# A spectral mixing kernel on one core: three weight transfers in one piece instead of three uneven ones

## The chip, the cores and the metric

The kernel runs on one core of a Trainium2 chip. The metric is the device time of one execution in microseconds (us); lower is better. The engines named below are TensorE (PE in the profile, PEld for its weight loads), VectorE (DVE), ScalarE (ACT), GpSimd (POOL) and SyncE (SP). Transfers between the chip's memory and the core run on 16 DMA engines, whichever engine issues them.

## The reference

Two stages, here cut to what they compute. There are B = 8 batches, S = 576 positions, 8 heads of 64 columns (D = 512 columns together) and 64 modes.

```
scores = q k^T / 8, masked: heads 0-3 see the last 32 positions,
                            heads 4-7 the earlier positions that are equal modulo 32
x = softmax(scores) v, heads side by side                    # [8, 576, 512]
X = rfft(x, axis=1)[:, :64]
Y[b, m, :] = X[b, m, :] @ (w_r[m] + i w_i[m])                # 64 complex matrices of 512 x 512
u = x + irfft(Y, n=576)
out = u + relu(u @ w_ch)                                     # float32
```

The weights w_r and w_i are 2 x 64 x 512 x 512 float32 numbers, 134 MB of the 163 MB that are read from memory. Each is used once, for eight batches.

## The kernel before

All transfers of inputs are issued by POOL, which turns float32 into float16 on the way. The attention's inputs come first and in between; the weights follow in an order that is written out (`ORDER`): 56 modes of the second half of the input channels, 48 modes of the first half, then the remaining 8 and 16. `w_fetch` loads two modes of one half at a time into a tile `wt` of 128 partitions: partitions 0 to 63 take the real parts (w_r, line 185), partitions 64 to 127 the imaginary parts (w_i, line 185), each as one transfer of 64 partitions x 2 modes x 2048 numbers, 512 KB as written. The first transfers of each half and the last four modes are loaded one mode at a time (line 189). There are five rotating buffers for these tiles and three more in places that are free for a while.

`i` is the position in `ORDER`, counted in modes, and steps by two. At three of these positions, 44, 74 and 102, the kernel before loads the real parts in three transfers (line 181) that share out the 64 partitions as the table `UNEVEN` says: 35, 18 and 11; 5, 33 and 26; 18, 35 and 11.

POOL's transfers take turns on eight semaphores, so that a transfer is issued after the one eight places before it has landed; a transfer into a buffer that was in use also waits for TensorE to be done with that buffer (`mode`, line 564). After every second mode, `mode` calls `w_fetch` for the next pair.

Attention is worked on in eight batches, first its strided heads, then its local heads, with the first modes spread between the local heads' steps. While the 48 modes that follow are worked off, `turn` and `premix` transpose x and multiply it by w_ch ahead of time, since u @ w_ch = x @ w_ch + irfft(Y) @ w_ch. In the last 24 modes one step of a list `late` follows each mode: `renew` adds what the first three of the four groups of 16 modes bring to x and to x @ w_ch (lines 894, 906 and 707 on TensorE, lines 250 and 911 on ScalarE and VectorE). When the last mode is done, the fourth group is added (line 965), and the rows go out through ScalarE, VectorE and SP.

The order of the work on each engine is the order in which it is written; no scheduler changes it.

Of the kernel before, what the change touches and what calls it, by code (L numbers as in the profile page):

```python
# [56 lines left out]
def kernel(  # L57
# [10 lines left out]
    nc = tc.nc  # L68
# [79 lines left out]
    SPLIT1, SPLIT0 = 56, 48  # L148
    ORDER = [(1, m) for m in range(SPLIT1)] + [(0, m) for m in range(SPLIT0)]
    ORDER += [(1, m) for m in range(SPLIT1, NM)] + [(0, m) for m in range(SPLIT0, NM)]  # L150
    UNEVEN = {44: (35, 18, 11), 74: (5, 33, 26), 102: (18, 35, 11)}
    w_tiles = []
    w_chs = {}
    w_ch = big.tile([128, 4, DM], F16, name="w_ch")
# [1 line left out]
    def w_fetch(n=1):  # L156
        for _ in range(n):
            i = len(w_tiles)
            if i >= 2 * NM:
                return  # L160
            half, m = ORDER[i]
            if i // 2 in GUEST:
                wt = big.tile([128, 2, 4, DM], F16, tag=GUEST[i // 2], name="wt")
            else:
                wt = pw.tile([128, 2, 4, DM], F16, tag="w", name="wt")
            single = []
            for ri, src in enumerate((moe_w_r, moe_w_i)):
                dst = wt[ds(64 * ri, 64)]
                rows = src[m : m + 2, ds(256 * half, 256), :].rearrange(
                    "m (p c) e -> p m (c e)", c=4  # L170
                )
                dst = dst.rearrange("p m c e -> p m (c e)")


                ones = range(2)
                if ri and not m:
                    ones = [1]
                elif i in UNEVEN and not ri:
                    a = 0
                    for n in UNEVEN[i]:  # L180
                        nc.gpsimd.dma_start(dst[a : a + n], rows[a : a + n])
                        a += n
                    continue
                elif i < 2 * NM - 4:
                    nc.gpsimd.dma_start(dst, rows)  # L185
                    continue
                single += [(j, ri, dst[:, j], rows[:, j]) for j in ones]
            for _, _, to, rows in sorted(single, key=lambda x: x[:2]):
                nc.gpsimd.dma_start(to, rows)
            w_tiles.extend((wt[:, 0], wt[:, 1]))  # L190
# [362 lines left out]
    def mode(slot, m):  # L553
# [17 lines left out]
        if m % 2 and (slot or m // 2 not in GUEST):  # L571
            w_fetch()
# [144 lines left out]
    strided_tokens()  # L717
    load_str(2, 2)
    w_fetch()

    def str_front(b):
# [35 lines left out]
    for b in range(B):  # L757
        if b in (1, 3):
            load_str(b + 3, 2)
        load_loc(*[(), (), (), (), (0,), (1, 2), (3,), (4, 5)][b])  # L760
        w_fetch([2, 1, 1, 1, 1, 1, 0, 0][b])
        front = str_front(b + 1) if b + 1 < B else loc_front(0)
        for t in range(6):
            str_scores(b, t)
            if b > 0:
                if t < 2:
                    str_values(b - 1, 4 + t)
                elif t == 2:
                    dft(b - 1, 1)
            if t >= 2:  # L770
                str_values(b, t - 2)
            for w in front[SPLIT[t] : SPLIT[t + 1]]:
                w()
        if b == 1:
            nc.vector.memset(PL[:, 0:PS0], 0.0)
            fourier(0)
# [8 lines left out]
    for b in range(B):  # L785
# [12 lines left out]
        n = 0  # L798
        nm = NMODES[b]
        for mi in range(nm):  # L800
# [3 lines left out]
            n = upto  # L804
# [66 lines left out]
    n = 0  # L871
    for m in range(SPLIT0):
# [4 lines left out]
        n = upto  # L877
# [125 lines left out]
    n = 0  # L1003
    NL = len(rest) - 2
    for i, (slot, m) in enumerate(rest):
# [4 lines left out]
        n = upto  # L1010
# [76 lines left out]
```

## Time and profile before

| | us |
|---|---|
| median of three runs | 434.12 (433.67 to 434.50) |
| profiled execution | 434.12 |
| its span, from the first to the last instruction | 432.3 |

| engine | busy us (share of the span) |
|---|---|
| TensorE, matmuls | 348.7 (81%) |
| VectorE | 236.3 (55%) |
| ScalarE | 203.5 (47%) |
| POOL | 111.0 (26%) |

The core read 162.8 MB and wrote 9.4 MB; the DMA engines moved 91.78 MB as written, since the weights shrink to float16 on the way.

How to read it: the slices cut the span in 40 equal parts of 10.8 us, and a digit is the busy share in tenths. The chain is followed back from the last instruction, at each step to what released it. A line of the POOL timeline gives the start of an issue, how long POOL was at it, what it moves, and in brackets how long POOL stood still before it and what ended that. The trace also has a record for each packet and for each landing of a transfer on one of the 16 DMA engines.

### The profile page before, as it was taken

The numbers are of one execution on the slowest core, as the hardware profiler recorded it, in microseconds if no ns is written. First come the engines' busy times: TensorE is split into PE (matmuls) and PEld (weight loads), VectorE is DVE, ScalarE is ACT, GpSimd is POOL, SyncE is SP. The second block draws the span as 40 slices with busy tenths as digits, with TensorE's granted clock in tenths as the row PEclk, the third lists the DMA queues.
The fourth block names the chain that finished last, engine by engine and source line by source line (L and its number), as shares of the span: only waits on it lengthen the run. The fifth ranks groups of instructions, "written<-read, shape, count | busy, mean of one in ns | idle before, by whom it ended". The sixth has DMA issues, their size and how long they took to land.

```text
span 432.3 us, 12283 instructions
## 1 busy us (share of the span) xinstructions
PE 348.7 (81%) x5420; PEld 240.0 (56%) x5420; DVE 236.3 (55%) x461; ACT 203.5 (47%) x357; POOL 111.0 (26%) x197
## 2 busy tenths in 40 slices
PE   2978788779897888898477878787887888988994
PEld 2867676558676666666344545455554544444331
DVE  3887878844533424533104244865783474444685
ACT  1776778636545345546141222522441453432773
POOL 8333332323332222232222222222223222110000
PEclk9997999968968869969655578999898989899997
DMA  8999999999999999999999999999999999991698
GB/s 151 211 211 213 214 212 212 212 210 212 214 212 213 214 213 214 212 213 214 211 214 214 213 213 215 213 213 213 213 214 211 214 213 214 213 200 30 219 355 300
DMA packets 30900, 91.78 MB, mean 212 GB/s; under 512 B 4416, under 2 KB 5184, under 8 KB 30848
## 3 DMA queue, kind: packets, MB, share of 16 engines
q0 software_dynamic: 25120, 81.28, 95.1%
q1 hardware_dynamic: 5216, 9.52, 6.2%
q8 instruction: 42, 0.69, 0.6%
q10 hardware_dynamic: 512, 0.21, 0.2%
q14 instruction: 10, 0.08, 0.0%
HBM read 162.83 MB, written 9.44 MB: 398 GB/s over the span
## 4 chain that ended last, share of the span: by engine, by line
DMA 59%; PE 21%; DVE 9%; ACT 5%; issue 4%; POOL 1%; DVEq 0%; POOLq 0%; ACTq 0%
DMA wt<-in_moe_w_i_dram 46%; DMA wt<-in_moe_w_r_dram 11%; DVE kz L282 3%; PE y L564 2%; DVE xb L240 2%; PE v L942 2%; PE u L952 2%; PE sc L531 2%; ACT X L250 2%; PE v L965 1%; DMA ring<-in_q_dram 1%; PE tp L412 1%; ACT v L250 1%; DVE rec L239 1%; ACT PL L377 1%
## 5 line engine op out<-in xcount | busy, mean ns | idle before, releaser
L564 PE MATMUL y<-X,wt 128*128 128x16 f16 (+1 forms) x2048 | 82.4, 192 | 37.1 <-DMA wt<-in_moe_w_i_dram 35.3
L564 PEld LDWEIGHTS <-wt 128*128 128x128 f16 (+1 forms) x2048 | 72.9, 102 | 52.0 <-issue 45.3
L185 POOL DMA_DIRECT2D wt<-in_moe_w_r_dram x59 | 34.6, 586 | 128.2 <-PE y L564 50.9
L185 POOL DMA_DIRECT2D wt<-in_moe_w_i_dram x60 | 35.3, 588 | 66.9 <-DMA wt<-in_moe_w_i_dram 47.6
L673 ACT ACTIVATE v<-sc 128x512 f16<-128x512 f32 x32 | 19.1, 597 | 67.5 <-PE sc L664 67.4
L488 ACT ACTIVATE PL<-sc 128x480 f16<-128x480 f32 (+1 forms) x48 | 27.4, 579 | 33.1 <-PE sc L474 32.7
L664 PE MATMUL sc<-w_cp,xT 128*128 128x512 f16 x128 | 40.0, 440 | 1.3 <-DVE xT L637 1.3
L674 DVE COPY xo<-tp 128x512 f16<-128x512 f16 x32 | 22.1, 691 | 34.1 <-PE tp L672 34.0
L240 DVE TENSOR_TENSOR xb<-av,rec 90x256 f16<-90x256 f32 (+2 forms) x80 | 36.0, 450 | 2.8
L239 DVE RECIPROCAL rec<-av 90x4 f32<-90x4 f32 (+2 forms) x80 | 14.6, 183 | 35.2 <-PE av L503 24.8
L419 DVE COPY qT<-tp 128x576 f16<-128x576 f16 x16 | 12.0, 758 | 39.1 <-PE tp L412 36.2
L911 DVE TENSOR_TENSOR xo<-u,xo 128x1024 f16<-128x1024 f32 x16 | 19.6, 1225 | 16.9 <-PE u L707 16.9
L250 ACT ACTIVATE v<-tp 128x640 f16<-128x640 f16 (+1 forms) x24 | 19.4, 807 | 18.8 <-PE tp L446 16.3
L412 PE MATMUL tp<-cI_s,ring 64*64 64x64 f16 x864 | 25.1, 205 | 1.2 <-DVE qT L419 0.6
L377 ACT ACTIVATE PL<-sc 90x360 f16<-90x360 f32 (+1 forms) x48 | 22.7, 490 | 7.1 <-PE sc L370 6.5
L250 ACT ACTIVATE v<-v 128x1024 f16<-128x1024 f32 x16 | 16.4, 1023 | 19.6 <-PE v L707 19.6
L987 DVE TENSOR_TENSOR osb<-u,rl 128x1024 f32<-128x1024 f32 (+1 forms) x21 | 22.2, 1071 | 5.5 <-PE u L965 3.4
L458 PE MATMUL sc<-cMl_s,cI_s 128*128 128x480 f16 (+1 forms) x48 | 21.1, 440 | 3.2 <-ACT X L250 1.6
L412 PEld LDWEIGHTS <-ring 64*64 64x64 f16 x864 | 19.6, 118 | 6.2 <-issue 2.8
L275 PE MATMUL tp<-cI_s,ring 72*128 72x72 f16 x256 | 15.6, 208 | 8.6 <-DMA ring<-in_v_dram 6.9
L531 PEld LDWEIGHTS <-xb 108*128 108x128 f16 (+2 forms) x176 | 15.3, 106 | 12.0 <-DVE xb L240 7.2
L979 ACT ACTIVATE rl<-v 128x1024 f32<-128x1024 f32 (+1 forms) x21 | 18.8, 901 | 6.6 <-PE u L965 4.1
(135 smaller groups left out, 705.5 us busy)
## 6 DMA issues: line engine op xcount, KB each, us to landing
wt<-in_moe_w_i_dram POOLq DMA_DIRECT2D x60, 512.0 KB, 18.8
wt<-in_moe_w_r_dram POOLq DMA_DIRECT2D x59, 512.0 KB, 18.0
out_dram<-osb SPq DMA_DIRECT2D x15, 512.0 KB, 3.2
ring<-in_v_dram POOLq DMA_DIRECT2D x8, 288.0 KB, 13.3
ring<-in_q_dram POOLq DMA_DIRECT2D x8, 288.0 KB, 13.6
ring<-in_k_dram POOLq DMA_DIRECT2D x8, 288.0 KB, 13.1
ring<-in_v_dram POOLq DMA_DIRECT2D x3, 512.0 KB, 14.7
ring<-in_q_dram POOLq DMA_DIRECT2D x3, 512.0 KB, 14.6
```

What stands on the lines that cost most here:

```text
L185: nc.gpsimd.dma_start(dst, rows)
L240: nc.vector.tensor_tensor(out=dst, in0=val.rearrange("p h (q c) -> p h c q", c=4), in1=rec[0:n, 0:pieces] .to_broadcast((n, pieces, 64)) . ...
L250: nc.scalar.activation(out=out, in_=in_, func=ACTF.Copy)
L377: nc.scalar.activation(out=PS[0:n, ds(POFF[t], 4 * n)], in_=scp[0:n, 0 : 4 * n], func=ACTF.Exp, scale=SCALE,)
L412: nc.tensor.transpose(tp[ds(64 * hp, 64), ds(64 * i, 64)], qn[ds(64 * hp, 64), ds(64 * (9 * g + i), 64)], idn[ds(64 * hp, 64), ds(64 * hp, ...
L458: nc.tensor.matmul(scp[:, 0 : n * times].rearrange("p (h x) -> p h x", h=times), idn, mask_rows("cMl", n, times), start=True, stop=False,)
L488: nc.scalar.activation(out=dst, in_=src, func=ACTF.Exp, scale=SCALE)
L531: nc.tensor.matmul(xp[:, ds(192 * cp, 192)].rearrange("p (f m) -> p f m", f=3), xb[b][0:n, base + t, ds(128 * cp, 128)], F[0:n, :, t, :], ...
L564: nc.tensor.matmul(yv[:, mi, e, :], wt[pr, XC[c], ds(128 * e, 128)], Xh[half][pr, c, :, :, m], start=(c == 0), stop=(c == 3),)
L664: nc.tensor.matmul(vp, xT[:, ch], w_chs["cp"][:, ch, :], start=(ch == 0), stop=(ch == 3),)
L674: nc.vector.tensor_copy(out=xo.rearrange("p (h q c) -> p h q c", h=2, c=4), in_=tp[:, 0:512].rearrange("p (h c q) -> p h q c", h=2, c=4),)
L987: nc.vector.tensor_tensor(out=osb[:, j], in0=up[:, j], in1=rl[:, j], op=AluOp.add)
```

## The change

The table `UNEVEN` and the branch that used it go. The real parts at positions 44, 74 and 102 are loaded by line 185 like all the others: one transfer of 64 partitions instead of three. POOL issues 184 transfers instead of 190; the bytes, the tiles, their order and the instructions of all other engines are the same.

```
-    UNEVEN = {44: (35, 18, 11), 74: (5, 33, 26), 102: (18, 35, 11)}
...
                 ones = range(2)
                 if ri and not m:
                     ones = [1]
-                elif i in UNEVEN and not ri:
-                    a = 0
-                    for n in UNEVEN[i]:
-                        nc.gpsimd.dma_start(dst[a : a + n], rows[a : a + n])
-                        a += n
-                    continue
                 elif i < 2 * NM - 4:
                     nc.gpsimd.dma_start(dst, rows)
                     continue
```

## The prediction

> **What bounds the kernel now.** I read the page's slices and queues first, then the chain of waits, the waits of TensorE, the issues on the POOL timeline, and last the trace's landing events.
>
> ```profile
> span 432.3 us, 12283 instructions
> DMA  8999999999999999999999999999999999991698
> q0 software_dynamic: 25120, 81.28, 95.1%
> q8 instruction: 42, 0.69, 0.6%
> DMA 59%; PE 21%; DVE 9%; ACT 5%; issue 4%; POOL 1%; DVEq 0%; POOLq 0%; ACTq 0%
> ```
>
> The DMA row is at 9 from the second slice to the thirty-sixth: from 10 to about 390 us the weight stream never pauses, and 59% of the chain that ended last is a transfer. The small queue q8 moves instructions over the same 16 engines in 42 packets of 16 KB; 0.6% of 16 x 432.3 us is 41 us, so about 1 us each.
>
> TensorE's waits, then two pieces of the chain in order of time:
>
> ```profile
> PE y L564 <- DMA wt<-in_moe_w_i_dram: 35.3, 33, 4.5
> ```
>
> ```profile
> 365.82 19.38 DMA wt<-in_moe_w_i_dram
> 385.33 0.64 PE y L564 x16
> ```
>
> TensorE waits 35.3 us for weights in 33 places. The last of these waits ends at 385.3 us, with the landing of the transfer issued at 365.82. After that TensorE and ScalarE have their own work in a row: the last mode's matmuls start at 396.92 although the last weights land at 395.08, and the rest of the span is a fixed tail. So the span moves with the landing at 385.20.
>
> The three places that the change touches look alike on the POOL timeline; the first:
>
> ```profile
> 163.77 0.58 POOL L185 DMA_DIRECT2D wt<-in_moe_w_i_dram  x1 [0.43 <-DMA wt<-in_moe_w_i_dram]
> 166.56 0.71 POOL L181 DMA_DIRECT2D wt<-in_moe_w_r_dram  x1 [2.21 <-PE y L564]
> 168.70 0.60 POOL L181 DMA_DIRECT2D wt<-in_moe_w_r_dram  x1 [1.44 <-DMA wt<-in_moe_w_i_dram]
> 171.15 0.56 POOL L181 DMA_DIRECT2D wt<-in_moe_w_r_dram  x1 [1.84 <-DMA wt<-in_moe_w_r_dram]
> 173.61 0.60 POOL L185 DMA_DIRECT2D wt<-in_moe_w_i_dram  x1 [1.91 <-DMA wt<-in_moe_w_i_dram]
> ```
>
> A transfer is issued when the one eight before it has landed, so eight are on the way, and each lands some 18 us after its issue.
>
> A transfer's time is that of its slowest DMA engine. The trace holds sixteen landing events for each transfer, one per engine (us of the span):
>
> ```
> transfer (512 KB each)                  first    third-last  last two
> imag rows before the first uneven pair  178.87   182.58      183.01 183.15
> imag rows of that pair                  183.13   187.02      188.52 188.63
> imag rows before the second             253.26   258.73      259.95 260.00
> imag rows of that pair                  258.03   262.72      265.32 265.38
> imag rows before the third              321.49   328.17      330.89 330.96
> imag rows of that pair                  325.91   332.15      335.88 336.05
> the one that the chain waits for        376.35   381.33      385.04 385.20
> ```
>
> In undisturbed stretches the last landing advances by 2.458 us per transfer (16 in a row take 39.32): the slowest engine always has work. 128 rows of 4 KB over 16 engines are 8 each, so a row takes about 0.305 us. At the end two engines stand 3.7 us behind the other fourteen.
>
> **The change part by part.** It removes nine issues at line 181 and adds three at line 185: six fewer on the POOL queue, 6 x 0.6 = 3.6 us of POOL. Behind each stand only later weight issues, which wait 1.4 to 2.2 us for a landing anyway; worth nothing. If that cover went, a delayed issue would still have seven transfers, some 17 us, queued before it. Bytes and order stay. Nothing is added that waits; a 512 KB issue takes one of eight places where three pieces took three, so more bytes can be on the way. That helps engines that run ahead, not the one that is late: nothing again.
>
> The Trainium skill ("DMA: Bandwidth & Descriptors", section "Anatomy of one DMA") puts a fixed 2.0 us on each transfer; by it, six fewer would be an estimated 12 us. The landings speak against it here: in the first group the second and third piece land 0.20 and 0.30 us after the one before. A fixed cost with eight on the way is hidden, and the sum goes without it.
>
> What is left is which engine moves which row. A 64-partition transfer gives each engine 8 rows. The same page (section "Why a DMA increments its semaphore by 16 and not by 1") says that the number of engines is the largest divisor up to 16 of the partition count, taken in turn from a moving position: 35, 18 and 11 would use 7, 9 and 11. The page of the profile agrees: q0 has 25120 packets, and 18496 data rows of 4 KB or 1 KB, 3072 of 2304 B and 190 x 16 semaphore writes leave 512, which is what idle engines writing one empty packet per missing row would make, summed over the nine pieces and the twelve 8-partition loads. Without the page: the landings below show unequal shares.
>
> First estimate, from the last landings alone. A pair of transfers should take 2 x 2.458 = 4.92 us; the three uneven pairs take 5.48, 5.38 and 5.09. Together 15.95 - 14.75 = 1.2 us too much.
>
> Second estimate, engine by engine. The two late engines are not those that were last before the first uneven pair; followed back, they landed there at 182.4. From there to the landing at 385.20 stand 79 full transfers, one half and w_ch: 79 x 2.458 + 1.24 + 2.6 = 198.0 us. They took 202.8. Of the 4.8 more, two instruction packets explain 2.3 (each time one runs, one engine's landing steps back by 1.07 to 1.25 us, and eight engines take them in turn); 2.5 is left, 8 rows of 0.305. So the uneven pieces gave these two engines eight rows more than an even split. After the change they land 2.5 us earlier. Who is late next? The engines that were last at 183.15, which now get back the rows that the pieces had spared them: 183.15 + 198.0 + 2.3 = 383.4. So the landing moves from 385.20 to 383.4: -1.8 us.
>
> The two differ because the first compares each group with itself and misses that other engines were relieved. I take -1.6, nearer to the second, which follows engines; its bounds are -1.2 (the first) and -2.5 (if nothing else comes late). Further fetches late in the stream could cost the new last engine 1.1 us, but after 385 the weights have 396.92 - 395.08 = 1.8 us to spare, so this costs nothing; if that cover were gone it would leave -0.5.
>
> Does TensorE follow? In the stretch before the last wait it has room:
>
> ```profile
> 380.42 0.64 PE L564 MATMUL y<-X,wt 128*128 128x16 f16 x16 [0.83 <-DMA wt<-in_moe_w_i_dram]
> 385.33 0.64 PE L564 MATMUL y<-X,wt 128*128 128x16 f16 x16 [0.93 <-DMA wt<-in_moe_w_i_dram]
> ```
>
> It idles 0.8 to 0.9 of every 4.9 us, and earlier waits are up to 4.5; all of them end earlier together, so a gain is passed on whole. The profiled execution has 434.12 us beside a span of 432.3, 1.8 around it, and is itself the median of 433.67 to 434.5. 434.12 - 1.6 = 432.5.
>
> **The rivals.** *No change (433.3 to 435.0).* Either the stage is paced by TensorE and ScalarE, whose work between two pairs (two late steps of about 2.15 us) fills 4.3 of 4.92 us, or the new last engine draws a fetch before 385 (-1.8 + 1.1 = -0.7). Against the first: the wait of 0.93 at 385.33. For the second: the fetches go round eight engines and their places shift with the instructions.
>
> *Slower: the pieces usually relieve the engines that fetch instructions.* Before the first uneven pair, the landings fall into eight engines within 0.95 us of the first and eight that are 2.5 to 4.3 behind: these carry the fetches. In the profiled execution six of them were spared rows and two were loaded. If the place at which the turn starts differs from execution to execution, others spare all eight. The last landing there is that of the new last engine less 6 to 8 rows, so the even split costs 7 x 0.305 = +2.1 us, at most 2.4: 436.2. It decides where the timed executions start their turn elsewhere than the profiled one. Against it: the profiled time is the median, and three runs within 0.83 us leave no room for a 4 us spread, unless each is a mean over many starts, and then the sign turns back.
>
> *The pieces do nothing* (engines shared evenly in spite of them): 434.1, part of no change. Against it: 5.48 where 4.92 is due.
>
> **How the numbers follow.** The gain has 0.58 and its own range is 431.7 to 433.2; no change 0.16; slower 0.26, at 435.0 to 436.5. A measurement of this kernel tells about 0.2%, or 0.87 us, from no change. The gain's cases nearly all pass this; of no change half a tenth does on each side, and the slower case passes it whole: faster 0.59, same 0.14, slower 0.27. The range goes from 431.4 to 435.9, leaving out the gain's far end (0.05) and the upper half of the slower case (0.13).
>
> **What would show it.** Right: nine L181 issues gone, the last landing advancing by 2.46 us per transfer through all three pairs, no pair of engines far behind at the end (last minus third-last under 1 us instead of 3.7), and the wait at 385.33 ending near 383.7. Wrong: last landings no earlier at 385, or TensorE's waits in the last stage gone without a shorter span; or before's own time differing between executions by several us.

## The result, and the profile after

The kernel after takes 432.26 us (median of 4 runs, 431.95 to 433.08), the kernel before 434.03 us beside it (4 runs, 433.67 to 434.50). The ratio is 0.9962, with a 95% interval of 0.9944 to 0.9979: faster, by 1.8 us or 0.4%. 432.5 was predicted.

The slices and queues of the kernel after, from the first part of its profile:

```profile
span 430.2 us, 12274 instructions
DMA  8999999999999999999999999999999999992698
q0 software_dynamic: 24704, 81.28, 95.3%
DMA 69%; PE 20%; DVE 5%; issue 2%; ACT 2%; POOL 1%; DVEq 0%; ACTq 0%; POOLq 0%
```

The stream is as dense as before and still bounds the kernel. Queue q0 (packets, MB, share of 16 engines) moves the same bytes in 416 packets fewer. That is 6 x 16 = 96 semaphore writes of the six transfers that are gone, and 320 others: the number of rows that some engine lacked in the nine uneven pieces, (16 - 7) x 10 for a piece of 35 partitions on 7 engines and so on. All 416 are packets of 4 bytes in the trace, and the count fits an idle engine that writes one empty packet for each row of a busy one.

The POOL timeline where the first uneven pair was (start, time at the issue, in brackets the standstill before it):

```profile
163.59 0.58 POOL L178 DMA_DIRECT2D wt<-in_moe_w_i_dram  x1 [1.37 <-DMA wt<-in_moe_w_i_dram]
166.36 0.58 POOL L178 DMA_DIRECT2D wt<-in_moe_w_r_dram  x1 [2.20 <-PE tp L405]
168.56 0.58 POOL L178 DMA_DIRECT2D wt<-in_moe_w_i_dram  x1 [1.61 <-DMA wt<-in_moe_w_i_dram]
```

One issue stands where three did. Now the waits of TensorE for weights (total, times, longest), two pieces of the chain in order of time, and the two matmul groups of the PE timeline that answer to those shown of before:

```profile
PE y L557 <- DMA wt<-in_moe_w_i_dram: 35.7, 30, 4.2
```

```profile
363.79 19.38 DMA wt<-in_moe_w_i_dram
383.16 0.14 issue
383.30 0.64 PE y L557 x16
```

```profile
378.45 0.64 PE L557 MATMUL y<-X,wt 128*128 128x16 f16 x16 [0.90 <-DMA wt<-in_moe_w_i_dram]
383.30 0.64 PE L557 MATMUL y<-X,wt 128*128 128x16 f16 x16 [0.85 <-DMA wt<-in_moe_w_i_dram]
```

The total of the waits is what it was. The stream still ends last at each of them; each only ends earlier. The last one ends at 383.30 in place of 385.33, since the weights land at 383.16 in place of 385.20. The sixteen landings of that transfer, sorted (us of the span). It has eight more behind it, and the expectations below call it the eighth from the end:

```
before  376.35 376.50 378.14 378.28 379.46 380.57 380.89 380.96
        381.02 381.14 381.29 381.31 381.32 381.33 385.04 385.20
after   376.26 376.71 376.84 376.97 377.38 377.72 377.92 378.98
        382.30 382.32 382.61 382.67 382.70 382.73 382.85 383.16
```

Two engines that stood 3.7 us behind all others are gone. In their place eight stand level, within 0.9 us, and the other eight are 3 to 7 us ahead of them. The eight that are late are those that carry the instruction packets of queue q8; below, the two groups are called the late and the early half.

### The profile page after: what moved, and what is told of

The parts are those of the page before. It is cut to its first block, busy times and chain, and to the rows that moved or that the text cites. A ratio compares the mean times of both kernels' runs of the same rounds, so it can differ in the third digit from the quotient of the medians.

```text
span 430.2 us, 12274 instructions
## 1 busy us (share of the span) xinstructions
PE 344.0 (80%) x5420; PEld 238.3 (55%) x5420; DVE 236.3 (55%) x461; ACT 203.5 (47%) x357; POOL 107.4 (25%) x191
## 4 chain that ended last, share of the span: by engine, by line
DMA 69%; PE 20%; DVE 5%; issue 2%; ACT 2%; POOL 1%; DVEq 0%; ACTq 0%; POOLq 0%
DMA wt<-in_moe_w_i_dram 52%; DMA ring<-in_q_dram 7%; DMA ring<-in_v_dram 4%; DMA wt<-in_moe_w_r_dram 4%; PE y L557 3%; PE v L935 2%; PE u L945 2%; DMA ring<-in_k_dram 2%; PE v L958 1%; DVE yy L692 1%; PE sc L524 1%; PE sc L657 1%; DVE xb L233 1%; PE tp L405 1%; ACT v L243 1%
## 5 line engine op out<-in xcount | busy, mean ns | idle before, releaser
L178 POOL DMA_DIRECT2D wt<-in_moe_w_r_dram x62 | 36.4, 587 | 155.8 <-PE y L557 75.4
L657 PE MATMUL sc<-w_cp,xT 128*128 128x512 f16 x128 | 38.3, 425 | 1.3 <-DVE xT L630 1.3
```

The source lines that it names most:

```text
L657: nc.tensor.matmul(vp, xT[:, ch], w_chs["cp"][:, ch, :], start=(ch == 0), stop=(ch == 3),)
```

## The experiments

The theory (T): the time follows the slowest of 16 engines, and what the uneven pieces did is decided by *which* engines got more rows, so by the size of a piece and by the place in turn at which it began. The rivals: the number of transfers matters (R1); the place doesn't move, or moves otherwise (R2). Small extra loads serve as tools below: they move almost nothing, but may move the place. A load of k x n lines takes k partitions with n contiguous lines for each. "Before" and "after" stand for the two kernels. Their data go to a scratch tile, or to where w_ch is loaded later.

**Even shares in as many transfers (even3, before with other pieces).**

```
-    UNEVEN = {44: (35, 18, 11), 74: (5, 33, 26), 102: (18, 35, 11)}
+    UNEVEN = {44: (32, 16, 16), 74: (32, 16, 16), 102: (32, 16, 16)}
```

> The kernel before, with the three uneven pairs cut into pieces of 32, 16 and 16 partitions: still three transfers each and 190 in all, but all 16 engines move 2 + 1 + 1 partitions of each, as in one piece. Theory (unequal shares made two engines late): as the kernel after, 432.3 us (431.9 to 433.0), and at the end all eight late engines within 1 us of one another. Rival (the six extra transfers cost the time, by themselves or through the eight places on the way): as the kernel before, 434.0.

Measured: 432.69 us (6 runs, 432.06 to 433.09), ratio to before 0.9960 (0.9947 to 0.9974), the same gain as after. The eight late engines land within 1.45 us of one another at the transfer that the chain waits for, not within 1 us. The end of the last wait in its chain, for a profiled execution of 433.09 us, the slowest of the six:

```profile
364.38 19.38 DMA wt<-in_moe_w_i_dram
383.76 0.14 issue
383.90 0.64 PE y L564 x16
```

All 190 transfers are still there, and the gain is too, so R1 is out. The shares were the cost.

**One small load ahead, 8 x 1 lines (turn8).** Before, and ahead of the first weight transfer:

```
+    scr = big.tile([16, 64], F16, name="scr")
+    nc.gpsimd.dma_start(scr[0:8], q[0, 0, 0:8, :])
```

> The kernel before plus one tiny transfer of 8 partitions x 64 numbers near the start, which should move the place where the turn of engines starts on by eight; the uneven pieces are unchanged. Theory: the two halves of the engines change roles. The two engines that were 8 rows over are now spared about 8, and of the six instruction-fetching engines that were spared most get 8 to 10 rows more than an even split: the last landing of the stage comes 2.4 to 3.0 us after that of the kernel after, 385.6 to 386.2 instead of 383.2, so 434.8 to 435.4 us, with three or more engines late instead of two. Rival (which engine moves what does not matter, or the place is not carried from one transfer to the next): 434.0, and two late engines.

Measured: 434.33 us (10 runs), ratio 1.0004 (0.9994 to 1.0014), the last two landings at 384.09 and 385.06, the third-last at 381.23. Nothing moved. T in this form missed.

**Three more with such loads, ahead of the weights and behind the last uneven pair (turn_0_13, turn_8_5, turn_4_9).** `spin(k)` is such a load of k lines; the numbers in the names are the two k.

> The kernel before plus one tiny transfer of 13 partitions x 64 numbers after the last uneven pair. The engine counts of all transfers on fewer than 16 engines then add up to a multiple of 16, so that an execution would end at the place of the turn at which it began. Theory A (the place is carried on from transfer to transfer, and from one execution to the next): the uneven pieces fall on other engines than in the kernel before; other engines are late at the end, and the time changes by at least 1 us: 430.5 to 432 if all fetching engines are spared, 435 to 436 if two of them take 10 rows more. Theory B (the place does not depend on what went before): 434.1 and the same two late engines, the ones whose landings step back with the fetches at about 230 and 240 us.

> As the run before, but a tiny transfer of 8 partitions ahead of the first uneven pair and one of 5 after the last: again a multiple of 16 in all, with the uneven pieces half a turn further on than there. Theory A: the engines that are loaded and spared change roles against the run before, so the two times differ, by 1 us or more, and one of them is not 434.1. Theory B: both 434.1 with the same two late engines.

> As the two runs before with 4 partitions ahead and 9 after: the uneven pieces a quarter of a turn further on than with nothing ahead. Theory A: a third pattern; one step away from the place of the kernel before, with two or three late engines, 433.5 to 435.5 us. Theory B: 434.1 and the same two late engines.

Measured: 434.08, 433.83 and 434.50 us (10 runs each), ratios 1.0000, 1.0001 and 1.0011 (the last from 1.0001 to 1.0022). In all three the same picture of two late engines, the last of them 2.8 to 3.1 us behind the third-last. Loads of one line per partition don't move the place, whatever their number: R2 was right for them.

**Who carries a small load (map and map15).** After, with sixteen loads behind the pairs at positions 20 to 50: of 1 x 2 lines in map, of 15 lines of 2 KB in map15.

> The kernel after plus sixteen one-partition loads (two rows of 2 KB each), one after each pair from position 20 to 50, into a place that is overwritten later. Theory: each runs on a single engine, the next in turn, so each engine takes one of them, and the packets show which places of the turn belong to engines that fetch instructions: two or three in the first seven or eight places counted from the start and five or six in the others, 0.3 us more per engine, 432.6 us in all. Rival (shares are spread over all engines, or the place is not carried on): no engine, or always the same one, steps back.

> The kernel after plus sixteen loads of 15 partitions x one row of 2 KB, one after each pair from position 20 to 50, into a place that is overwritten later. Each leaves one engine out. Theory A: the engine left out moves on by one place each time, through all sixteen. Theory B: always the same engine is left out. In both 0.2 us for each row on a late engine, 434 to 435 us in all, as the run with one-partition loads gave 434.8.

Measured: in map all 32 packets ran on the same two engines, both of the early half. In map15 the same engine was left out every time; its landing, counted from the earliest, fell from 1.23 us by some 0.16 a load to 0. So these loads, of one line per partition and on a single partition, always began at one fixed engine. The Trainium skill ("DMA: Bandwidth & Descriptors", section "Why a DMA increments its semaphore by 16 and not by 1") names an exception that may be this one: some direct copies are shared out over all 16 engines, and only a transfer over fewer engines begins at the moving place. The page doesn't say which copies these are; that loads of one line per partition are among them is a reading of the two runs here.

The two kernels took 434.82 and 434.86 us (one run each). At about 205 us their early engines stand still until the late ones have nearly caught up, by some 4 to 5 us, which those of after don't; so their times say nothing of the ring. The halt comes from the tools: the small loads write where w_ch is loaded later, so POOL holds the load of w_ch back until the last of them has landed, 9.73 us in map and 10.33 us in map15, and issues no weights meanwhile. In after it waits 1.81 us there.

**The same with two lines per partition, as the weight pieces have (map15_2).**

```
+                    if ri and i in range(20, 52, 2):
+                        p, h = divmod((i - 20) // 2, 2)
+                        nc.gpsimd.dma_start(
+                            w_ch[15 * p : 15 * p + 15, 2 * h : 2 * h + 2],
+                            rows[0:15, :, 0:512],
+                        )
```

> The whole transfers, plus sixteen small loads of 15 x 2 lines of 1 KB after pairs 20 to 50 (their values go where the channel weights are fetched later). Theory that a transfer cut into several lines per partition moves the place in turn: each load leaves out one engine, and the next load the next one (15 engines on, 16 in the ring: one step back each), so that after sixteen loads each engine was left out once and the landings of the sixteen engines stand to each other as without the loads, 0.1 to 0.2 us of work per load later for all. Theory that every small transfer begins at the same engine, as the loads of one line per partition did: the same engine is left out sixteen times, and its landings move ahead of the others' by some 0.16 us a load. Time by either: 434.0 to 435.5 us.

Measured: 435.33 us (one run, with that halt, 10.40 us of POOL). Each load shows 30 packets of 1 KB in the records, two for each of 15 engines, and the engine that is left out is another each time, one step back in the ring. Read from the packets' starts beside the landings of the transfer before, it belongs to the early half (E) or to the late half (L), which carries the instruction packets:

```
load           1  2  3  4  5  6  7  8  9 10 11 12 13 14 15 16
left out is    E  L  L  L  L  L  L  E  E  L  L  E  E  E  E  E
place in ring 15 14 13 12 11 10  9  8  7  6  5  4  3  2  1  0
```

(The fourth was at the early end of its half then and went to the late one with its next instruction packet.) Places are counted from the one where the first uneven piece begins. So the eight engines that carry instructions are 5, 6 and 9 to 14. This is the whole map. With 7, 9 and 11 engines for 35, 18 and 11 partitions, 5, 11 and 13 for the second group and 9, 7 and 11 for the third, the pieces of before give places 5 and 6 eight rows too many and the other six instruction engines six or eight too few: the two late engines of the profile, counted and not fitted.

**Moving the place with loads of that shape (place8, place0).** Before, with 8 x 2 lines ahead of the weights and 5 x 2 behind the last pair (place8), or 13 x 2 behind it alone (place0).

```
+        nc.gpsimd.dma_start(
+            scr[0:k], q[0, 0:2, 0:k, :].rearrange("h s d -> s h d")
+        )
```

> The kernel before, plus one small load of 8 x 2 lines ahead of the first weight transfer and one of 5 x 2 behind the last uneven pair. Theory that transfers of several lines per partition move the place in turn: the three uneven pairs begin 8 engines on, the two engines that carried eight rows too many now have fewer than their share and others have two to ten too many; the last landings of the eighth transfer from the end are those of other engines, its last less its third-last landing under 2 us, the time 433.5 to 435.5 us. Theory that the place isn't moved by small transfers of any shape: the same two engines land last, last less third-last 2.8 to 3.9 us, 434.1 us.

> The kernel before, plus one small load of 13 x 2 lines behind the last uneven pair, none ahead. Moved place: the place at the end of an execution is 16 engines on from its start instead of 3; if an execution begins where the last one ended, the two late engines may be others than before in the profiled one, and all executions of this kernel are alike, so that their times spread less than those of the kernel before (433.4 to 435.1 us). Place that begins anew with each execution, or isn't moved: the same two engines land last, last less third-last 2.8 to 3.9 us, 434.1 us with the same spread.

Measured: place8 435.39 us (5 runs, 435.04 to 435.95), ratio 1.0036 (1.0022 to 1.0050); place0 433.80 us (10 runs), ratio 0.9996 (0.9987 to 1.0005). Six engines land last in place8 where two did, at 386.07 to 386.98, the next at 381.08: by the map, six of the eight now get eight or ten rows too many. The end of the last wait in its chain:

```profile
367.56 19.41 DMA wt<-in_moe_w_i_dram
386.98 0.14 issue
387.11 0.64 PE y L571 x16
```

In place0 the picture is that of before: two engines land last, at 384.56 and 384.90, and the third-last at 381.41. A load behind the last pair alone costs nothing there, so what costs 1.4 us in place8 is the load of 8 x 2 lines of 128 bytes ahead. (A load behind the last pair takes one of the eight places on the way. In place8 the engines furthest ahead run dry there for want of issued transfers: the first landing of the next transfer comes 5.39 us after that of the small load, at 329.14. The late ones have work all along.) The place begins anew with each execution, as bal4 shows more sharply below.

**Pieces chosen by the map (bal4).** Before, with pieces that take six rows from each of the eight instruction engines:

```
+    UNEVEN = {44: (7, 52, 5), 60: (6, 50, 8), 80: (6, 56, 2), 100: (24, 13, 27)}
```

> The kernel before with other pieces: 7, 52, 5 and 6, 50, 8 and 6, 56, 2 and 24, 13, 27 partitions for the real parts of four pairs, where before has three pairs in pieces. Theory that the place in turn moves with these transfers, and that the run with the loads of 15 x 2 lines shows the ring (counted from the place where the first uneven piece begins, the engines that also carry instruction packets are 5, 6, and 9 to 14): these eight carry six lines of 4 KB less each than with whole transfers, the other eight up to eight more, so the eight late engines land the eighth transfer from the end 1.8 us earlier than in the kernel after, at 380.5 to 381.4 us in place of 382.3 to 383.2, level with the highest of the others, and TensorE follows: 430.3 to 431.2 us, faster than the kernel after by 1 to 2 us. Rival, that the ring is read wrongly or the balance of the engines no longer ends last: 432.3 us or more.

Measured: 430.71 us (5 runs, 430.25 to 431.22), ratio to before 0.9930 (0.9916 to 0.9944). This beats both kernels; after, measured beside before in another comparison, had 0.9962 (0.9944 to 0.9979), so the two intervals only touch. The medians differ by 1.5 us, and the slowest run of bal4 is faster than the fastest of after (431.95). The landing at 381.68 is 0.3 us later than expected, the time is within what was expected. Queue q0 has 25120 packets, as many as before, so the number of packets isn't what costs. Its span and the end of its last wait:

```profile
span 428.7 us, 12287 instructions
362.30 19.38 DMA wt<-in_moe_w_i_dram
381.68 0.14 issue
381.81 0.64 PE y L564 x16
```

**The same pieces, eight places on (bal4_8).** bal4 and one load of 8 x 2 lines ahead of the weights.

> The pieces of bal4 unchanged, and one small load of 8 x 2 lines ahead of the first weight transfer, so that every piece begins eight engines on. If what bal4 gains is the place of its pieces over the ring, two engines that carry instruction packets now get eight lines too many and one gets six, others of the eight six too few: the last landings of the eighth transfer from the end are again near 385 us, three at the most over 384, and the time is 433.6 to 434.6 us, some 3 us over bal4 with the same pieces. If bal4 gains through the number or the size of its pieces, the time stays at 430.3 to 431.2 us and the last landings at 381 to 382 us.

Measured: 434.60 us (9 runs, 433.97 to 436.34), ratio to before 1.0022 (1.0011 to 1.0033), 3.9 us over bal4.

```profile
span 432.2 us, 12288 instructions
365.91 19.38 DMA wt<-in_moe_w_i_dram
385.29 0.04 issue
385.33 0.65 PE y L569 x16
```

The last four landings are 382.78, 384.98, 385.15 and 385.29. By the map, of the eight engines one has its even share, one six rows too many and two eight. With the same pieces at another place, all of bal4's gain is gone.

The map's count beside the landings, all for that same transfer, with eight more behind it:

```
kernel   most rows over an     x 0.305 us   last      against   span less
         instruction engine's               landing   after     that landing
         even share
bal4         -6                 -1.8        381.68     -1.5       47.0
after         0                  0          383.16      0         47.0
even3         0                  0          383.76     +0.6       47.5
before       +8                 +2.4        385.20     +2.0       47.1
bal4_8       +8                 +2.4        385.29     +2.1       46.9
place8      +10                 +3.1        386.98     +3.8       47.0
```

## Why the prediction was right

**The bound.** Right: in these six kernels the span is the last landing plus 46.9 to 47.5 us, so the tail is fixed and TensorE passes a gain or a loss on whole. The wait at 385.33 ends at 383.30 (near 383.7 was said), with 0.85 us of idle time before it.

**Six issues fewer worth nothing.** Right, shown by even3. A fixed cost per transfer was rightly left out of the sum: even3 keeps all 190 transfers and has the whole gain.

**Which engine moves which row.** Right, and now shown: the eight rows too many that were worked back from the landings are the eight that the map counts. The last landing advances by 4.97, 4.97 and 4.85 us through the three former uneven pairs, where it was 5.48, 5.38 and 5.09 and two even transfers take 4.92.

**The sum.** The new last engine was put at 383.4 and landed at 383.16; -1.8 us was worked out and -2.0 came for the landing. The step that was a little off is the shading to -1.6 towards the first estimate: that one compares each group with itself and can't see which engines are relieved, so it deserved no weight. The medians give -1.8 us.

**Later fetches.** As said: one engine falls back late in the stream, by some 1.4 us (at the last transfer it lands at 394.20, the next at 392.75), under the cover of the last weights, and costs nothing.

**The rivals.** *No change* fell: the spread of the last three landings is 0.43 us, and none of the late engines had drawn a packet more than the others by then. Forty instruction packets had run, five for each of the eight, and the forty-first began at 389.4; the prediction had left open when it would come, so that part is luck. *Slower, since the pieces usually relieve the engines that fetch* fell at its condition. It needed a place that differs from execution to execution. The place begins anew in each: place8 and bal4_8 show that another place makes 1.4 and 3.9 us, while the five runs of bal4, whose pieces would move the place by 9 of 16 from one execution to the next, lie within 1.0 us. Its mechanism is real, though, and its sign too: pieces that spare all eight do beat the even split, which is bal4. *The pieces do nothing* fell with even3.

**What stays open.** place8's last landing is 0.7 us later than the map counts. bal4 has not levelled all engines: its sixteen landings still reach from 376.57 to 381.68, so a better table may be worth up to another 1.5 us, an estimate from the mean of the sixteen, 380.1. A table of pieces holds only while the place and the instruction engines stay as they are; what moves them between builds wasn't tried.

## What to carry to other kernels

Where a stream of transfers bounds a kernel, look at the sixteen landings of a late transfer and not at the mean of the engines: the time is that of the last, and the distance between the last and the rest is what can be won. An uneven split isn't good or bad by itself; the same sizes gained 3.3 us over before or lost 0.7 with their place in the ring, and a tiny load far ahead, with several lines per partition, can move it. If the map isn't known, split evenly.

## What the runs showed of the hardware

- Eight of the 16 DMA engines carried the instruction packets, one at a time in turn: 42 packets of 16 KB, each setting one engine back by 1.07 to 1.25 us. At the end of a stream of 380 us that made a difference of some 6 us between the halves in after.
- In these runs, a POOL load with several lines per partition began where the last such one ended and moved the place by the number of engines it used (15 x 2 lines left out another engine each time, one step back). A load with one line per partition, or on one partition alone, always began at the same engine (15 lines left out the same one in 16 of 16 loads) and didn't move the place (turn8 and the three like it, ratios 1.0000 to 1.0011). The place is the same at the start of each execution: another place makes 3.9 us, and the five runs of bal4 lie within 1.0 us.
- By the count of packets, an engine that a transfer doesn't use still takes part in it, with an empty packet for every row of a busy engine: 416 packets fewer in q0 after, 96 of them semaphore writes.
